# Attention and SwiGLU block on one core: the reciprocal of the softmax sums, on VectorE or on GpSimd by place in the program

## The chip, the cores and the metric

One core of a Trainium2 chip runs the whole program. The metric is the device time of one execution in microseconds, as a median over runs; lower is better. Engines are named as the profile names them: PE is TensorE, DVE is VectorE, ACT is ScalarE, POOL is GpSimd, SP is SyncE, which here only issues DMAs.

## The reference

A block with adaptive layer norm: 32-head softmax attention over 2048 tokens of width 512 (16 columns a head), then a SwiGLU feed-forward of width 1792.

```python
q, k, v = qkv[0], qkv[1], qkv[2]
scores = jnp.einsum("bhqd,bhkd->bhqk", q, k) * scale
p = _softmax(scores, axis=-1)
o = jnp.einsum("bhqk,bhkd->bhqd", p, v)
x = x + ga * (o.reshape(B, S, D) @ wo)
h = _layernorm(x, axis=-1) * (1 + cb) + sb
x = x + gb * ((_silu(h @ w_gate) * (h @ w_up)) @ w_down)
```

The change concerns one division: the row sum of the softmax, by which each row of `o` is divided.

## The kernel before

**Units and steps.** Attention is cut into 32 units (`NU`): unit `u` is one group of four heads against one chunk of 512 queries, eight units a chunk, four chunks. A unit has 16 steps, one per tile of 128 keys. In a step PE makes four score matmuls (`score`, L571), ACT turns each into exponentials (L573), and two steps later PE multiplies them with the values (`pv_step`, L586). The values carry a column of ones, so the sums of the softmax come out as a 17th row of each head's product. Ahead of the scores by 20 steps (`LEAD` is 21), PE makes four more score matmuls per step in the other orientation (`max_one`, L523), and DVE reduces each from PSUM to its row maximum (L525). They go over four banks in turn, so that PE can be some banks ahead of DVE and no more. After 64 of them `max_rows` (steps without filler) or `max_turned` (steps with filler) turns a unit's maxima into rows that are written into the unit's query operand by small DMAs from SP (`qop<-mr`, L541, or `qop<-turned`, L562); the first score of that unit reads them.

**Plain steps and steps with filler.** The program's order is written out by hand. `plain` emits steps that hold attention alone and sets `beside = False`; `filled` emits steps with matmuls of the previous chunk's output projection and feed-forward between those of attention (L789) and sets `beside = True`. Plain steps run from the beginning of attention to step 147, then around the chunk ends up to steps 275 and 403, in a stretch of 36 after the third chunk's output projection, and three at a time ahead of a chunk's last down projection.

**The end of a unit.** `close_unit` (L929) queues the division of a finished unit, one part per step:

- `out_a`, L597: SP sends the four rows of sums from `o` to `dn`, spread over 128 partitions by 16 columns.
- `out_b`, L601 and L602: DVE takes the reciprocal of `dn` in place; SP writes it to `d_dr` in DRAM.
- `out_r`, L607: SP reads `d_dr` back as `rb`, each row broadcast over 32 partitions. This DMA waits for the landing of the one before it.
- `out_c`, L613 and L614: POOL multiplies `o` by `rb` to `on` and sends it to `o_dr`.

All engines execute their own list in order, and so does SP: a DMA that waits for a semaphore holds back the DMAs behind it, `qop<-mr` of a later unit among them.

**POOL's other work.** In the first eight units POOL also splits the feed-forward's weights in two parts (`split_weights`, three pieces a unit, L644 to L686) and issues half of the loads of the key operand (`kop<-kd`) and of the query operand (`qop<-qd`) for the unit three ahead. In later units it makes the second parts of the hidden activations (L870, L871).

The steps of the end of a unit, as `close_unit` sets them:

```python
i0 = i if u % NG == NG - 1 else i + 3
at(i0 + 3, lambda: res.__setitem__(u, out_b(u, nc.sync, *res[u])))
at(i0 + 4, lambda: res.__setitem__(u, out_r(u, nc.sync, *res[u])))
at(i0 + 5, lambda: out_c(u, nc.gpsimd, nc.gpsimd, *res.pop(u)))
```

Of the kernel before, what the change touches and what calls it, by code (L numbers as in the profile page):

```python
# [11 lines left out]
F32 = mybir.dt.float32  # L12
# [4 lines left out]
ALU = mybir.AluOpType  # L17
# [4 lines left out]
P = 128  # L22
# [10 lines left out]
NU = NG * NC  # L33
# [70 lines left out]
def block_kernel(ctx, tc, x, wqkv, wo, w_gate, w_up, w_down, c, w_mod, out):  # L104
    nc = tc.nc
# [386 lines left out]
    pb = ctx.enter_context(tc.tile_pool(name="pb", bufs=2, reuse_waits="tile"))  # L492
# [100 lines left out]
    def out_a(u, eng):  # L593
# [3 lines left out]
        eng.dma_start(dn, o[16:P:32, :].rearrange("h (b e) -> h b e", e=16))  # L597
        return o, dn

    def out_b(u, eng, o, dn):  # L600
        nc.vector.reciprocal(dn, dn)  # L601
        eng.dma_start(d_dr[u].rearrange("h (b e) -> (h b) e", e=16), dn)  # L602
        return o,

# [324 lines left out]
    def close_unit(u, i):  # L929

        if u == NU - 1:
            res[u] = out_a(u, nc.scalar)
            return
        res[u] = out_a(u, nc.sync)
        if u + 3 < NU:
            load_k(u + 3)
            load_q(u + 3)
# [4 lines that stand above are left out]
        if u % NG == NG - 1:  # L942
            if u // NG:
                at(i + 4, lambda: begin(u // NG))
                at(i + 5, lambda: chunks[u // NG].load_wo())
            at(i + 7, lambda: chunks[u // NG].load_o(nc.gpsimd))
            at(i + 9, lambda: chunks[u // NG].split_o())
# [5 lines left out]
    beside = True  # L953
# [184 lines left out]
    for t in range(4):  # L1138
        out_terms(ch, t, banks[t], range(NK - 1))
    on = out_b(NU - 1, nc.scalar, *res[NU - 1])  # L1140
    on = out_r(NU - 1, nc.scalar, *on)
    out_c(NU - 1, nc.scalar, nc.vector, *on)
# [47 lines left out]
```

## Time and profile before

| What | Value |
|---|---|
| Median of 3 runs | 1826.32 us (1826.1 to 1827.04) |
| The profiled execution | 1826.86 us, its span 1825.0 us |
| PE busy | 1816.3 us (100%) |
| DVE busy | 1521.2 us (83%) |
| ACT busy | 1248.0 us (68%) |
| POOL busy | 459.9 us (25%) |
| Chain that ended last | PE 83%, DVE 14%, ACT 1% |
| Granted PE clock | 1.000 over the span |

Busy time of PE is modelled from pipelined matmuls and is an average over stages with different limits; the stage is read with the timeline, the waits and the busy time by window. A line such as L525 is a line of the kernel before.

### The profile page before, as it was taken

The page shows a single profiled execution, that of the slowest core. Times are in us where ns is not written, and L with a number is a line of the kernel's source. Part 1 is how long each engine was busy: PE and PEld are TensorE (multiplying, and loading weights), DVE is VectorE, ACT ScalarE, POOL GpSimd, SP SyncE. Part 2 cuts the span into 40 slices and gives each one's busy share as a digit, 9 for nine tenths or more (in the row PEclk, how much of TensorE's full clock was granted, in tenths as well). Part 3 has the DMA queues.
Part 4 walks back from the last instruction along what each step waited for, and adds up shares of the span by engine and source line. Part 5 has one row for each costly group of instructions (what it writes and reads, how often), then busy time and mean ns, then how long its engine had stood idle before and what let it go on. Part 6 is the DMA issues. An engine that isn't in the chain of part 4 may idle for free.

```text
span 1825.0 us, 40961 instructions
## 1 busy us (share of the span) xinstructions
PE 1816.3 (100%) x16904; PEld 1202.5 (66%) x16904; DVE 1521.2 (83%) x2554; ACT 1248.0 (68%) x2358; POOL 459.9 (25%) x538
## 2 busy tenths in 40 slices
PE   9999999999999999999999999999999999999999
PEld 7876444444465777776565777776564577777887
DVE  5578999999999888888999888889999988832544
ACT  4223888888888766777888767767888876673211
POOL 3612544556223111111123111111113011131200
PEclk9999999999999999999999999999999999999999
DMA  9883876667845444453544554444643536333742
GB/s 307 288 232 138 203 199 172 179 167 199 207 81 125 103 122 143 115 149 70 145 110 105 141 125 118 122 118 91 161 80 57 116 90 157 134 123 120 279 167 108
DMA packets 80486, 267.62 MB, mean 147 GB/s; under 512 B 19604, under 2 KB 24212, under 8 KB 59620
## 3 DMA queue, kind: packets, MB, share of 16 engines
q1 hardware_dynamic: 61324, 179.71, 34.0%
q0 software_dynamic: 18288, 84.49, 19.5%
q8 instruction: 133, 2.18, 0.5%
q10 hardware_dynamic: 688, 0.80, 0.1%
q14 instruction: 53, 0.43, 0.1%
HBM read 201.85 MB, written 62.13 MB: 145 GB/s over the span
## 4 chain that ended last, share of the span: by engine, by line
PE 83%; DVE 14%; ACT 1%; DMA 0%; issue 0%; SPq 0%; DVEq 0%
PE bank L586 21%; PE bank L789 20%; PE bank L571 14%; DVE mx L525 14%; PE bank L523 11%; PE bank L808 8%; PE bank L213 7%; PE bank L851 1%; PE bank L772 0%; DMA wm_ab<-in_w_mod 0%; PE bank L165 0%; ACT sq L832 0%; DVE v_flat L882 0%; PE bank L537 0%; SPq L261 0%
## 5 line engine op out<-in xcount | busy, mean ns | idle before, releaser
L525 DVE TENSOR_REDUCE mx<-bank 128x1 f32<-128x512 f32 x2048 | 1273.3, 681 | 111.0 <-PE bank L523 63.7
L571 PE MATMUL bank<-qop,kop 50*128 50x512 f32 x2048 | 729.7, 426 | 0.4 <-ACT pt__16494 L573 0.2
L523 PE MATMUL bank<-kop,qop 48*128 48x512 f32 x2048 | 724.6, 425 | 0.3
L571 PEld LDWEIGHTS bank<-qop,kop 50*128 50x128 f32 x2048 | 343.1, 184 | 168.9 <-issue 49.8
L523 PEld LDWEIGHTS bank<-kop,qop 48*128 48x128 f32 x2048 | 342.8, 184 | 106.2 <-DVE mx L525 62.1
L789 PE MATMUL bank<-act,wgu 64*128 64x512 f32 x1872 | 303.5, 392 | 0.0
L789 PEld LDWEIGHTS bank<-act,wgu 64*128 64x128 f32 x1872 | 199.4, 187 | 22.5
L613 POOL TENSOR_TENSOR on<-o,rb 128x512 f32<-128x512 f32 x31 | 39.9, 1286 | 507.8 <-DMA rb<-d_dr 359.0
L789 PE MATMUL bank<-wd,mid 64*128 64x512 f32 x912 | 131.6, 391 | 0.0
L870 POOL CAST mid<-m 128x512 fp32r<-128x512 f32 x40 | 24.4, 609 | 380.5 <-DVE m L868 273.7
L789 PEld LDWEIGHTS bank<-wd,mid 64*128 64x128 f32 x912 | 92.2, 186 | 11.2
L213 PE MATMUL bank<-hT,wqs 128*128 128x512 f32 x384 | 94.4, 397 | 0.4 <-DVE wqs L353 0.4
L866 DVE SCALAR_TENSOR_TENSOR q<-th,bank 128x512 f32<-128x512 f32 x56 | 38.3, 683 | 54.2 <-ACT th L862 54.2
L213 PEld LDWEIGHTS bank<-hT,wqs 128*128 128x128 f32 x384 | 70.6, 188 | 19.1 <-issue 3.2
L862 ACT ACTIVATE th<-bank 128x512 f32<-128x512 f32 x56 | 33.2, 594 | 57.9 <-PE bank L808 57.9
L882 DVE TENSOR_TENSOR x<-bank,x 128x512 f32<-128x512 f32 x84 | 53.9, 685 | 16.1 <-PE bank L789 16.1
L868 DVE TENSOR_TENSOR m<-bank,q 128x512 f32<-128x512 f32 x56 | 38.7, 692 | 21.7 <-PE bank L808 19.7
L871 POOL TENSOR_TENSOR mid<-m,mid 128x512 fp32r<-128x512 f32 x40 | 51.7, 1292 | 3.3
L808 PE MATMUL bank<-wd,mid 128*128 128x512 f32 x216 | 51.3, 393 | 0.0
L213 PE MATMUL bank<-wqs,hT 128*128 128x512 f32 x192 | 48.0, 398 | 0.0
L789 PE MATMUL bank<-wgu,act 64*128 64x512 f32 x288 | 47.6, 392 | 0.0
L808 PEld LDWEIGHTS bank<-wd,mid 128*128 128x128 f32 x216 | 40.4, 188 | 8.9
(6300 smaller groups left out, 5137.3 us busy)
## 6 DMA issues: line engine op xcount, KB each, us to landing
wgu<-gu_dr SPq DMA_DIRECT2D x48, 1024.0 KB
wd<-wd_dr SPq DMA_DIRECT2D x28, 1024.0 KB
kop<-kd SPq DMA_DIRECT2D x33, 768.0 KB
kop<-kd POOLq DMA_DIRECT2D x29, 768.0 KB, 8.8
gu_dr<-wgu POOLq DMA_DIRECT2D x14, 1024.0 KB, 13.6
kd<-prt SPq DMA_DIRECT2D x16, 512.0 KB
qd<-prt SPq DMA_DIRECT2D x16, 512.0 KB
kop<-gu_dr SPq DMA_DIRECT2D x8, 1024.0 KB
```

Source lines behind the costliest of these rows:

```text
L213: nc.tensor.matmul(pt, lhs(a, k), rhs(b, k), start=(n == 0), stop=(n == 3 * nk - 1))
L523: nc.tensor.matmul(pm, qop[u][rows, s, qt * P:(qt + 1) * P], kop[u % 3][rows, s, kc * CW:(kc + 1) * CW], start=True, stop=True)
L525: nc.vector.tensor_reduce(mx[u][:, b, s, qt, kc:kc + 1], pm, op=ALU.max, axis=AX.X)
L571: nc.tensor.matmul(sp, kop[u % 3][rows, h // 2, kt * P:(kt + 1) * P], qop[u][rows, h // 2, :], start=True, stop=True)
L586: nc.tensor.matmul(pv[u][32 * h:32 * h + 32, cols], v_flat[:, e0:e0 + 32], p_[h][:, cols], start=(kt == 0 and half == 0), stop=(kt == 15), ...
L613: mul.tensor_mul(on, o, rb)
L789: mm = nc.tensor.matmul(outs[e], lhs(e, a, k)[rows], rhs(b, k)[rows], start=(ph == 0 and j == 0), stop=(j == z and (ph == 1 or trade)), sk ...
L808: nc.tensor.matmul(outs[e], lhs(e, a, k), rhs(b, k), start=(j == 0), stop=(j == z))
L866: nc.vector.scalar_tensor_tensor(q, th, 1.0, outs[0], op0=ALU.add, op1=ALU.mult)
L868: nc.vector.tensor_mul(m32, outs[1], q)
L871: (nc.gpsimd if slow else nc.vector).tensor_sub(mid[:, 1, :], m32, mid[:, 0, :].bitcast(F32))
L882: nc.vector.tensor_add(ch.x2[:, t, :], outs[e], ch.x2[:, t, :])
```

## The change

In the changed program `out_b` has two branches. Where the unit's reciprocal falls in a step with filler, and for the last unit, DVE takes it as before. Where it falls in a plain step, POOL makes it in four instructions: a power of -1, and one Newton step (a product, `2 - product`, a product). A tile of exponents is filled once.

```diff
+    power = pb.tile([P, 16], F32, name="power", bufs=1)
+    nc.gpsimd.memset(power, -1.0)
+
     def out_b(u, eng, o, dn):
-        nc.vector.reciprocal(dn, dn)
+        if beside or u == NU - 1:
+            nc.vector.reciprocal(dn, dn)
+        else:
+            near, off = [pb.tile([P, 16], F32, name=f"near{k}", tag=f"near{k}", bufs=1) for k in range(2)]
+            nc.gpsimd.tensor_tensor(near, dn, power, op=ALU.pow)
+            nc.gpsimd.tensor_mul(off, dn, near)
+            nc.gpsimd.tensor_scalar(off, off, -1.0, 2.0, op0=ALU.mult, op1=ALU.add)
+            nc.gpsimd.tensor_mul(dn, near, off)
         eng.dma_start(d_dr[u].rearrange("h (b e) -> (h b) e", e=16), dn)
         return o,
```

Fourteen of the 32 reciprocals go to POOL: units 0 to 7, 14, 15, 22, 23, 25 and 26. From L602 on, lines carry numbers 10 higher in the changed program (L613 is L623). Three places show what moves.

DVE's list at the end of unit 0, as a piece of the difference (`bank_63` to `bank_66` are the banks of the maxima):

```order
 L525 TENSOR_REDUCE mx<-bank_64 128x1
 L525 TENSOR_REDUCE mx<-bank_65 128x1
-L601 RECIPROCAL dn<-dn 128x16
 L525 TENSOR_REDUCE mx<-bank_63 128x1
 L525 TENSOR_REDUCE mx<-bank_66 128x1
```

The reciprocal goes; the reductions around it keep their order.

POOL's list at the same place, before (the last store of a split weight, the division of unit 0, the next piece of weights):

```order
L652 DMA gu_dr<-wgu 128x2048
L613 TENSOR_TENSOR on<-o,rb 128x512
L614 DMA o_dr<-on 128x512
L644 DMA mid<-in_B_w_up 128x4x256
L686 TENSOR_TENSOR mid<-mid,gb_bc 128x1024
```

and in the changed program:

```order
L662 DMA gu_dr<-wgu 128x2048
L608 TENSOR_TENSOR near_2180<-dn,power 128x16
L609 TENSOR_TENSOR near_2181<-dn,near_2180 128x16
L610 TENSOR_SCALAR near_2181<-near_2181 128x16
L611 TENSOR_TENSOR dn<-near_2180,near_2181 128x16
L623 TENSOR_TENSOR on<-o,rb 128x512
L624 DMA o_dr<-on 128x512
L654 DMA mid<-in_B_w_up 128x4x256
L696 TENSOR_TENSOR mid<-mid,gb_bc 128x1024
```

The four instructions stand behind the weights of the unit and ahead of its division; nothing else on POOL moves.

SP's list at the end of unit 6, with the semaphores that each DMA waits for, before:

```order
L602 DMA d_dr<-dn 128x16 [waits DMAHW2_49,DVE_49]
L607 DMA rb<-d_dr 128x1x512 [waits DMAHW4_49,DMAHW2_49,Pool_49]
L541 DMA qop<-mr 2x8x128 [waits Activation_49]
L541 DMA qop<-mr 2x8x128 [waits DMAHW5_49]
```

and in the changed program:

```order
L612 DMA d_dr<-dn 128x16 [waits DMAHW2_49,Pool_49]
L617 DMA rb<-d_dr 128x1x512 [waits DMAHW4_49,DMAHW2_49]
L541 DMA qop<-mr 2x8x128 [waits Activation_49]
L541 DMA qop<-mr 2x8x128 [waits DMAHW5_49]
```

No DMA moves; the write of the reciprocals now waits for POOL where it waited for DVE, and the rows of maxima of unit 8 stand two DMAs behind it.

## Rows read from the trace of the kernel before

**Rows 1.** Busy time by window: us, PE, PEld, DVE, ACT, POOL busy (instructions), PEclk, DMA share, GB/s.

```profile
225.00:433.00 208.00, 207.94 (x2106) 100.86 (x2104) 207.81 (x357) 181.92 (x360) 102.19 (x105) 1.00 0.71 188
433.00:520.00 87.00, 86.95 (x884) 42.13 (x880) 86.80 (x150) 75.95 (x153) 37.61 (x39) 1.00 0.63 165
...
878.00:931.00 53.00, 52.80 (x543) 25.34 (x543) 52.83 (x90) 45.52 (x90) 15.09 (x20) 1.00 0.63 149
...
1283.00:1337.00 54.00, 53.80 (x536) 27.50 (x537) 53.27 (x91) 46.83 (x92) 14.00 (x18) 1.00 0.66 152
1394.00:1458.00 64.00, 63.90 (x641) 32.90 (x645) 63.22 (x109) 55.38 (x109) 6.04 (x8) 1.00 0.38 87
```

**Rows 2.** Waits in the plain stretch 225 to 520: us in total, times, longest.

```profile
PEld bank L523 <- DVE mx L525: 30.8, 89, 0.4
```

**Rows 3.** Timeline of DVE around unit 0's reciprocal: start us, us, engine, instruction.

```profile
231.01 0.24 DVE L601 RECIPROCAL dn<-dn 128x16 f32<-128x16 f32 x1
231.17 10.78 DVE L525 TENSOR_REDUCE mx<-bank 128x1 f32<-128x512 f32 x18
...
242.00 28.78 DVE L525 TENSOR_REDUCE mx<-bank 128x1 f32<-128x512 f32 x48
```

**Rows 4.** Chain of work through 225 to 350: start us, us, what.

```profile
231.09 0.16 DVE dn L601
```

**Rows 5.** Timeline of DVE around unit 14's reciprocal, in three plain steps between filled ones.

```profile
862.62 0.24 DVE L601 RECIPROCAL dn<-dn 128x16 f32<-128x16 f32 x1
862.78 5.68 DVE L525 TENSOR_REDUCE mx<-bank 128x1 f32<-128x512 f32 x9
868.70 2.06 DVE L525 TENSOR_REDUCE mx<-bank 128x1 f32<-128x512 f32 x3 [0.24 <-PE bank L523]
```

**Rows 6.** Timeline of POOL at the ends of units 0, 5 and 6.

```profile
223.35 0.59 POOL L652 DMA_DIRECT2D gu_dr<-wgu  x1 [0.30 <-POOL wgu L649]
240.90 1.27 POOL L613 TENSOR_TENSOR on<-o,rb 128x512 f32<-128x512 f32 x1 [16.96 <-DMA rb<-d_dr]
...
422.00 0.59 POOL L652 DMA_DIRECT2D gu_dr<-wgu  x1 [0.30 <-POOL wgu L649]
...
465.88 2.37 POOL L686 TENSOR_TENSOR mid<-mid,gb_bc 128x1024 f32<-128x1024 f32 x1 [6.42 <-DMA mid<-in_B_w_down]
...
472.12 0.60 POOL L652 DMA_DIRECT2D wd_dr<-wd  x1 [0.30 <-POOL wd L649]
476.40 1.28 POOL L613 TENSOR_TENSOR on<-o,rb 128x512 f32<-128x512 f32 x1 [3.69 <-DMA rb<-d_dr]
```

**Rows 7.** Timeline of POOL in a chain of small instructions (a layer norm's scale).

```profile
1370.14 0.20 POOL L755 TENSOR_TENSOR rs<-rs,mv 128x4 f32<-128x4 f32 x1
1370.44 0.20 POOL L756 TENSOR_SCALAR rs<-rs 128x4 f32<-128x4 f32 x1
```

**Rows 8.** Timeline of SP's DMAs at the ends of units 0, 5 and 6.

```profile
214.89 0.61 SPq L597 DMA_DIRECT2D dn<-o  x1
...
424.80 0.34 SPq L602 DMA_DIRECT2D d_dr<-dn  x1
432.82 0.56 SPq L607 DMA_DIRECT2D rb<-d_dr  x1
437.50 1.12 SPq L541 DMA_DIRECT2D qop<-mr  x2
...
463.17 0.34 SPq L602 DMA_DIRECT2D d_dr<-dn  x1
470.65 0.56 SPq L607 DMA_DIRECT2D rb<-d_dr  x1
477.12 1.40 SPq L541 DMA_DIRECT2D qop<-mr  x2
```

**Rows 9.** Score matmuls up to 481.2: count, ns min/median/max, first and last start.

```profile
L571 PE MATMUL bank<-qop,kop x513: 383/398/503, 167.5 to 480.9; 50*128 50x512 f32 x171
```

**Rows 10.** The dn tile, whole span: what its engine idled for, us, times.

```profile
  DMA dn<-o: 7.0, 1
```

## Prediction

> **What bounds the kernel now.** I read the page first, then the busy time by window, then DVE's timeline at each reciprocal. The page says PE 100% and DVE 83%, and its chain is mostly PE; that is an average over two kinds of stages. The windows tell them apart: from 225 to 433 us DVE is busy 207.81 of 208.00 us, and it is nearly as full in the other four windows of plain steps, 86.80 of 87, 52.83 of 53, 53.27 of 54 and 63.22 of 64 [rows 1]. PE reads as full in the same windows, but its ends are modelled; that it waits for DVE shows in the waits, where the weight load ahead of the matmul for the maxima stood 89 times behind a reduction between 225 and 520 us, 30.8 us in all [rows 2]. In plain steps, then, DVE sets the pace, at one reduction per 0.60 us (48 in 28.78 us) [rows 3]. In steps with filler PE sets it.
>
> What to see around unit 0's reciprocal: it starts at 231.01 us, and the next reduction at 231.17 us [rows 3]. Its 0.24 us of busy time overlap its neighbours, and it takes 0.16 us of DVE's time; the chain through this stretch also gives it 0.16 us [rows 4].
>
> **What the change removes.** Fourteen reciprocals leave DVE. Each is worth 0.16 us where DVE is the bound. By DVE's timeline that holds for twelve: units 0 to 7 lie in the first two windows, 15 and 23 in the next two, 25 and 26 in the last [rows 1]. Units 14 and 22 end in three plain steps between filled ones; there DVE runs out of work and waits 0.24 us for PE soon after unit 14's reciprocal [rows 5], and unit 22 repeats it. I count these two at nothing: PE hides them. So 12 x 0.16 = 1.92 us. PE is next in line in plain steps, and 0.16 us in a unit of some 38.5 us (64 reductions and two small instructions) is far less than what it waits for DVE per unit (30.8 us over 295 us, some 4 us a unit, of which a part overlaps matmuls in flight), so it does not take the gain back.
>
> **What it adds on POOL.** Four instructions on 128x16. For three of them the nearest rows are POOL's chain on 128x4: 0.20 us each, 0.30 us from start to start [rows 7]; the 128x512 product took 1.27 us [rows 6], so twelve more columns add 12 x (1.27 - 0.20) / 508 = 0.03 us. That makes 1.0 us for three. No row shows a power. Its lower bound is a product's 0.3 us; for the upper I take the 1.27 us of the product over 32 times the columns, though no row excludes more (a rival below). I take 0.5 us, nearer the 128x4 row because the tile is nearer to it: 1.5 us in all, between 1.3 and 2.3.
>
> This lies beside other work. After unit 0's last store, issued by 223.94 us, POOL did nothing until 240.90 us: it waited 16.96 us for `rb` [rows 6]. DVE came to the reciprocal at 231.01 us; POOL can begin it when the sums have landed, which is after their issue at 214.89 [rows 8] and, as DVE never waited for them but once at the very end of the program [rows 10], before 231.01. So the write of the reciprocals can leave up to 5.5 us sooner than before. At unit 5 POOL is free at 422.59 us, and done at 424.1 us, where SP issued at 424.80 [rows 6, 8]: no earlier, no later. The sooner division lets POOL begin the next unit's weights sooner, until the key loads wait for PE to let go of a buffer. It ends nothing that PE or DVE waits for, so I count it at nothing.
>
> The Trainium skill, GPSIMD Engine Reference, section 4.1, speaks against the move: elementwise work belongs on VectorE, since GpSimd is about twice as slow on two inputs. By that as a price for the path, four instructions at twice 0.24 us, fourteen times, would cost an estimated 27 us less the 2 saved; by the idle time in the rows it costs nothing.
>
> **The tight place is unit 6.** There POOL first waited 6.42 us for the last piece of weights, and was done with it only at 472.72 us, while DVE had let the reciprocals go at 463.17 us [rows 6, 8]. POOL's four instructions would end near 474.2 us, and the write would leave 11.3 us later than before. SP waits for its landing, which took 7.5 us from issue (463.17 to 470.65), then issues the read and only then the rows of maxima for unit 8. With the same landing time these leave at 474.5 + 7.5 + 0.6 = 482.6 us instead of 477.12 [rows 8]. The 513th score matmul, the first of unit 8, started at 480.9 us [rows 9], 2.4 us after the second of those DMAs was issued, and the landing takes part of that. So PE could stall by up to 5.5 us. Two things stand against it. If POOL enters unit 6 sooner by some 3 us (each earlier end sends its division 0 to 5.5 us sooner), 2.5 us are left; and DVE has filled banks to go on with, three at 0.6 us. I take 0 and keep 5.5 us for the range.
>
> **The sum.** 1826.86 us for the profiled execution less 1.92 is 1824.94. The median of the runs lies 0.54 us under that execution, so I forecast **1824.4 us**. That is 0.1%, and less than the 0.2% (3.65 us) that a measurement of this kernel can about tell from no change.
>
> **Rivals.**
>
> *Unit 6 is late.* For it: the 11.3 us above. Against it: POOL's head start. Price 1 to 5.5 us off the gain: 1825.4 to 1829.9, with 1827 as its middle.
>
> *Another bound takes over.* PE or ACT needs the 0.16 us itself, and DVE idles instead. For it: PE 207.94 of 208.00 us and the chain's share of PE. Against it: the waits for DVE. Time: 1826.3.
>
> *The power is slow, and the kernel slower than before.* The mechanism is one queue: a long power holds POOL, SP stands at the write of the reciprocals, and the rows of maxima behind it leave late, so that PE waits for the first score of a unit. At unit 5 the write could leave at 437.50 - 0.56 - 8.02 = 428.9 us without harm, 6.0 us after POOL is free (the 8.02 us are 424.80 to 432.82) [rows 6, 8]; unit 6 has nothing to spare. From about 6 us for the four instructions, unit 6 alone costs more than the change brings by over 3.65 us (10 us late, less 2 to 3 us that banks and head start absorb). At 10 us, unit 6 costs some 12 us, unit 5 some 3 and units 2 to 4 about 1 each: 18 - 1.9 gives 1842. Against it: the tile has only 16 columns. For it: no row shows a power on POOL, and one computed element by element could take this long. The Trainium skill, GPSIMD Engine Reference, section 2.1, adds that the first call of freshly loaded code pays about 6 us; no run here shows that for a power, paid once at unit 0 it would hide in the 17 us of idle time, and paid at every call it would make this rival true.
>
> *More than the sum.* Units 14 and 22 count too and each is worth its whole 0.24 us: 14 x 0.24 = 3.4 us, 1822.9; or the earlier divisions help somewhere I don't see.
>
> **How the numbers follow.** The forecast has a chance of 0.60, a late unit 6 of 0.17, another bound 0.10, the slow power 0.10, more than the sum 0.03. The range leaves out the slow power and a little of the others: from 1822.6 (the 3.4 us, and 0.3 us for the spread of runs) to 1829.4 (nearly all of unit 6's 5.5 us). Faster by over 0.2% needs a gain above 3.65 us, which only the last rival could give, with the edge of a noisy result: 0.04. Slower by over 0.2% is the slow power and a sliver of a late unit 6 with a cost that I undersized: 0.11. Within 0.2%: 0.85.
>
> **What would show it.** Right: in the changed profile 18 reciprocals of this tile remain on DVE, the reductions next to the removed ones follow at 0.6 us, DVE stays full in the plain windows, and the span from unit 0's end to unit 8's first score is shorter by 8 x 0.16 = 1.3 us, the rest being saved later. The four POOL instructions take 1.3 to 2.3 us. Wrong in the way of unit 6: the first score of unit 8 waits for `qop<-mr`, and DVE shows a gap of more than 1 us near 482 us. Wrong in the way of the power: one row on POOL of several us in each of the fourteen units, and waits for `qop<-mr` ahead of scores. If DVE shows new idle times after each removed reciprocal, another bound took over. If the time moves by more than 5.5 us with none of this, the prediction is wrong in a way that I have not seen.

## The result, and the profile after

The changed kernel takes 1834.38 us (median of six runs, 1832.39 to 1835.35) against 1826.99 us for the kernel before (six runs, 1826.1 to 1828.79): a ratio of 1.0038, 95% interval 1.0025 to 1.005. The change makes it slower by some 7 us. I had forecast 1824.4 us in a range up to 1829.4, so the time lies outside, on the side that I held unlikely. The profiled execution took 1832.39 us with a span of 1830.3 us; it is the fastest of the six.

On the page of the changed kernel (columns as described with its parts 1 and 5: busy us, share, instructions; then busy us, mean ns, idle before and its releaser):

```profile
PE 1817.3 (99%) x16904; PEld 1194.8 (65%) x16904; DVE 1521.1 (83%) x2540; ACT 1247.9 (68%) x2358; POOL 509.9 (28%) x595
...
L571 PE MATMUL bank<-qop,kop 50*128 50x512 f32 x2048 | 729.1, 425 | 3.6 <-DMA qop<-mr 3.1
...
L608 POOL TENSOR_TENSOR near<-dn,power 128x16 f32<-128x16 f32 x14 | 41.1, 2938 | 39.7 <-DMA dn<-o 39.6
```

PE fell from 100% of its span to 99%. Fourteen powers cost POOL 41.1 us, 2.94 us each. And the scores, L571, have an idle time that ended with `qop<-mr`: one wait of 3.1 us, the one that I had named as the sign of a late unit 6.

**Where the time went.** I subtracted the start of each instruction in the trace before from that of the same instruction in the trace after. This offset says in which stretch time was lost or won:

| Stretch of the changed kernel | Offset at its start | At its end |
|---|---|---|
| start to 20 us | 0 | +1.78 us |
| 20 to 464 us, units 0 to 5 | +1.78 | +0.92 |
| 464 to 494 us, end of unit 6, first scores of unit 8 | +0.92 | +5.55 |
| 494 to 1652 us | +5.55 | +4.52 |
| 1652 us to the end | +4.52 | +5.3 |

So the gain is there: 0.86 us over six units and 1.03 us in the rest, 1.9 us in all. Two places lose far more: the end of unit 6, 4.6 us, and the first 20 us of the program, 1.8 us. A further 0.8 us goes at the very end. DVE shows the gain as it was meant; in a plain stretch of the changed kernel (start us, us, instruction) its reductions run on where a reciprocal stood between them [rows 3]:

```profile
281.31 37.75 DVE L525 TENSOR_REDUCE mx<-bank 128x1 f32<-128x512 f32 x63
```

63 reductions in 37.75 us are 0.60 us each, with no gap.

**Unit 6.** POOL's timeline of the changed kernel at the ends of units 0 and 6 (last column: idle before, and its releaser) answers to [rows 6]:

```profile
225.54 2.96 POOL L608 TENSOR_TENSOR near<-dn,power 128x16 f32<-128x16 f32 x1
228.58 0.22 POOL L609 TENSOR_TENSOR near<-dn,near 128x16 f32<-128x16 f32 x1
228.90 0.20 POOL L610 TENSOR_SCALAR near<-near 128x16 f32<-128x16 f32 x1
229.19 0.22 POOL L611 TENSOR_TENSOR dn<-near,near 128x16 f32<-128x16 f32 x1
241.18 1.28 POOL L623 TENSOR_TENSOR on<-o,rb 128x512 f32<-128x512 f32 x1 [11.76 <-DMA rb<-d_dr]
...
466.19 2.37 POOL L696 TENSOR_TENSOR mid<-mid,gb_bc 128x1024 f32<-128x1024 f32 x1 [5.56 <-DMA mid<-in_B_w_down]
...
473.04 2.95 POOL L608 TENSOR_TENSOR near<-dn,power 128x16 f32<-128x16 f32 x1
...
476.67 0.22 POOL L611 TENSOR_TENSOR dn<-near,near 128x16 f32<-128x16 f32 x1
```

At unit 0 the four instructions take 3.9 us (225.54 to 229.41) and lie in idle time. At unit 6 POOL is held up by a load of weights, comes to the power at 473.04 us, and ends at 476.89. SP's timeline there, to be read beside [rows 8]:

```profile
476.92 0.34 SPq L612 DMA_DIRECT2D d_dr<-dn  x1
478.41 0.56 SPq L617 DMA_DIRECT2D rb<-d_dr  x1
479.03 1.13 SPq L541 DMA_DIRECT2D qop<-mr  x2
```

The write leaves 13.75 us later than before (463.17), its landing is waited for only 1.5 us instead of 7.5, and the rows of maxima leave 1.9 us later than before (477.12). Now they stand right behind the read `rb`, and the chain through this stretch shows what that does to them (start us, us, what):

```profile
479.63 5.28 DMA qop<-mr
484.92 0.14 issue
485.05 0.46 PE bank L571
```

They need 5.28 us from the issue of the second of them, and the first score of unit 8 starts at 485.05 us, where it started at 480.9 before [rows 9]. What follows stands in the windows (PE, PEld, DVE, ACT, POOL busy, then the granted clock, DMA share, GB/s). The kernel before:

```profile
10.00:20.00 10.00, 8.49 (x55) 5.26 (x54) 6.12 (x16) 6.20 (x11) 1.28 (x1) 1.00 0.94 302
...
484.00:488.00 4.00, 4.00 (x42) 2.11 (x40) 4.00 (x8) 3.80 (x9) 0.00 (x0) 1.00 1.10 331
```

and the changed one:

```profile
10.00:20.00 10.00, 8.70 (x48) 5.27 (x49) 3.90 (x12) 4.47 (x8) 1.27 (x1) 0.83 0.75 231
...
480.00:484.00 4.00, 1.98 (x22) 0.71 (x20) 3.27 (x6) 2.39 (x5) 0.00 (x0) 1.00 0.64 190
484.00:488.00 4.00, 2.95 (x22) 1.50 (x24) 0.69 (x1) 0.60 (x1) 1.54 (x2) 0.71 0.96 389
488.00:492.00 4.00, 4.00 (x32) 1.54 (x30) 3.85 (x7) 3.57 (x8) 1.55 (x3) 0.86 0.81 182
```

PE stands for 3.1 us, and behind the wait its granted clock is 0.71 and 0.86 over two windows, where it was 1.00; windows of 1 us add up to 3.4 us at 0.50, that is at 1.2 instead of 2.4 GHz. Of the 4.63 us lost here, 3.2 are lost when the first score starts (485.05 - 480.9 - 0.92), the other 1.4 after it.

**The start.** The first row of both fences is the other place: clock 1.00 before, 0.83 after. PE's timeline before,

```profile
1.19 9.05 PE L275 MATMUL bank<-busy 128*128 128x256 f32 x28 [1.19 <-DVE nil L278]
10.87 1.06 PE L286 MATMUL bank<-wm_ab,sc 128*32 128x512 f32 x8 [0.63 <-DMA wm_ab<-in_w_mod]
```

and after:

```profile
1.18 7.88 PE L275 MATMUL bank<-busy 128*128 128x256 f32 x28 [1.18 <-DVE nil L278]
11.12 1.89 PE L286 MATMUL bank<-wm_ab,sc 128*32 128x512 f32 x8 [2.06 <-DMA wm_ab<-in_w_mod]
```

L275 are matmuls that only keep PE busy until the first weights arrive (14 in the source, 28 in the trace). They ended 1.2 us sooner, PE then stood for 2.06 us, and the next eight matmuls took 1.89 us instead of 1.06.

### The profile page after: what moved, and what is told of

Same layout as the page of the kernel before. It is cut to its first block, busy times and chain, and to the rows that moved or that the text cites. A ratio compares the mean times of both kernels' runs of the same rounds, so it can differ in the third digit from the quotient of the medians.

```text
span 1830.3 us, 41008 instructions
## 1 busy us (share of the span) xinstructions
PE 1817.3 (99%) x16904; PEld 1194.8 (65%) x16904; DVE 1521.1 (83%) x2540; ACT 1247.9 (68%) x2358; POOL 509.9 (28%) x595
## 4 chain that ended last, share of the span: by engine, by line
PE 88%; DVE 8%; ACT 2%; DMA 2%; issue 0%; SPq 0%; DVEq 0%; ACTq 0%
PE bank L586 24%; PE bank L799 20%; PE bank L571 16%; PE bank L523 13%; DVE mx L525 8%; PE bank L213 7%; PE bank L818 7%; PE bank L782 0%; DMA wm_ab<-in_w_mod 0%; PE bank L165 0%; DMA qop<-mr 0%; DMA kop<-o_dr 0%; DMA rb<-d_dr 0%; ACT sq L842 0%; PE bank L861 0%
## 5 line engine op out<-in xcount | busy, mean ns | idle before, releaser
L571 PE MATMUL bank<-qop,kop 50*128 50x512 f32 x2048 | 729.1, 425 | 3.6 <-DMA qop<-mr 3.1
L571 PEld LDWEIGHTS bank<-qop,kop 50*128 50x128 f32 x2048 | 343.5, 184 | 175.5 <-issue 54.1
L623 POOL TENSOR_TENSOR on<-o,rb 128x512 f32<-128x512 f32 x31 | 39.9, 1288 | 413.2 <-DMA rb<-d_dr 316.4
L608 POOL TENSOR_TENSOR near<-dn,power 128x16 f32<-128x16 f32 x14 | 41.1, 2938 | 39.7 <-DMA dn<-o 39.6
```

Source lines behind the costliest of these rows:

```text
L571: nc.tensor.matmul(sp, kop[u % 3][rows, h // 2, kt * P:(kt + 1) * P], qop[u][rows, h // 2, :], start=True, stop=True)
L608: nc.gpsimd.tensor_tensor(near, dn, power, op=ALU.pow)
L623: mul.tensor_mul(on, o, rb)
```

## The experiments

Each ratio is to the kernel before, timed beside it, with its 95% interval. Edits are against the changed kernel unless the text says otherwise.

**The kernel before, again** (no edit to it).

> The kernel before, unchanged, to see what a measurement of no change looks like and how far the start of the program moves from one execution to the next. Theory Q (the loss is one queue at unit 6): ratio 1.000, its interval within 0.999 to 1.001; the first score matmul starts anywhere between 167 and 170 us, since the 1.7 us by which the changed program was late there are spread. Rival S (the changed program itself starts later, by 1.7 us in every execution): the first score of the copy starts at 167.5 us within 0.3 us.

Measured: 1826.65 against 1826.74 us, 0.9998 [0.999 to 1.0007]; clock 1.00 throughout, first score of the program at 166.9 us (169.2 in the changed kernel). A ratio can be told from 1 to about 0.1%. Between 20 and 1652 us this copy's offset moves by 0.4 us with no edit at all, so a gain of 1.9 us read from offsets is good to about half a microsecond. The first score lies outside what either theory had named.

**Unit 6 back on DVE.**

```diff
-        if beside or u == NU - 1:
+        if beside or u in (6, NU - 1):
```

> The change with unit 6 put back on DVE; thirteen reciprocals stay on POOL. Theory Q: no score waits for qop<-mr, PE's clock stays at 1.00 around 485 us, and eleven reciprocals of 0.16 us are saved: 1.8 us less than before, ratio 0.999. Rival S: about 1 us more than before, ratio 1.0005. Rival P (reciprocals on POOL cost time wherever they are made): still 4 us or more slower, ratio above 1.002.

Measured: 1825.48 against 1826.74 us, 0.9993 [0.9984 to 1.0002]. No score waits for `qop<-mr`, the write leaves at 462.27 us, the first score of unit 8 starts at 480.0. With one of the fourteen back on DVE the whole loss is gone; the other thirteen leave about 1 us of gain, not clear of no change. The start is not late here either, which the edit does not explain.

**Only unit 6 on POOL.**

```diff
-        if beside or u == NU - 1:
+        if u != 6:
```

> Unit 6 alone on POOL; the other 31 reciprocals stay on DVE. Theory Q: the whole loss is here, 4 to 6 us slower than before, ratio 1.0022 to 1.0033, with a wait of PE for qop<-mr of 3 us or more at the first score of unit 8 and a lower granted clock behind it. Rival P: a fourteenth of the loss, ratio within 1.000 to 1.001. Rival S: 2 us slower at most.

Measured: 1831.67 against 1826.74 us, 1.0026 [1.0013 to 1.0039]; the seven runs go from 1826.64, no loss at all, to 1836.87, which is the profiled one. Its chain:

```profile
474.23 2.97 POOL near L608
...
478.12 1.44 DMA d_dr<-dn
...
479.58 0.56 SPq L617
...
480.19 0.56 SPq L541
...
480.80 4.98 DMA qop<-mr
...
485.92 0.76 PE bank L571
```

This is the whole path in one piece: power, write, read, rows of maxima, score. And its windows:

```profile
484.00:488.00 4.00, 2.08 (x18) 0.91 (x18) 0.69 (x1) 0.60 (x1) 1.26 (x1) 0.65 0.98 373
488.00:492.00 4.00, 4.00 (x26) 1.83 (x20) 1.92 (x4) 1.65 (x4) 1.82 (x3) 0.50 0.73 213
492.00:496.00 4.00, 4.00 (x26) 1.44 (x28) 3.33 (x6) 3.54 (x7) 0.00 (x0) 0.50 1.02 156
496.00:500.00 4.00, 4.00 (x36) 1.72 (x30) 2.29 (x4) 1.70 (x4) 0.00 (x0) 0.64 1.07 154
```

The wait is 5.3 us; behind it PE runs at 0.50 of its clock for two whole windows and parts of two more, 13.7 us in all. The offset jumps by 10.7 us, twice the wait.

**Unit 6's write and read issued from POOL's queue.**

```diff
+        queue = nc.gpsimd if u == 6 else nc.sync
-        at(i0 + 3, lambda: res.__setitem__(u, out_b(u, nc.sync, *res[u])))
-        at(i0 + 4, lambda: res.__setitem__(u, out_r(u, nc.sync, *res[u])))
+        at(i0 + 3, lambda: res.__setitem__(u, out_b(u, queue, *res[u])))
+        at(i0 + 4, lambda: res.__setitem__(u, out_r(u, queue, *res[u])))
```

> The change, with the write d_dr<-dn and the read rb<-d_dr of unit 6 issued from POOL's queue instead of SP's; the four instructions on POOL stay where they are, as late as in the change. Theory Q: SP no longer stands at the write, the rows of maxima leave at about 478 us, no score waits, and 1.9 us are saved: ratio 0.999. Rival L (POOL's lateness itself is the loss, through the key loads and the division behind it, not SP's queue): a loss of 4 us or more stays, ratio above 1.002.

Measured: 1826.81 against 1826.74 us, 1.0 [0.9991 to 1.0009]. SP's timeline:

```profile
477.13 1.09 SPq L541 DMA_DIRECT2D qop<-mr  x2
```

The division of unit 6 itself is even later than in the change (its product at 489.15 us against 484.61), but the rows of maxima leave as in the kernel before, at 477.13, and no score waits. So nobody needs the quotient soon; what hurts is what stands behind it on SP. The 1.9 us that were to be saved besides do not show in the ratio.

**Only the read moved to POOL's queue.** In the last line of the program above, `nc.gpsimd if u == 6 else nc.sync` for `out_r` alone.

> The change, with the read rb<-d_dr of unit 6 alone issued from POOL's queue; the write stays on SP, behind POOL's four instructions, so SP stands there as long as in the change. Theory R (the rows of maxima are late because the read stands ahead of them on SP's queue and its transfer has to end first): they leave at about 479 us as before, land within 2.5 us, PE waits less than 1 us, ratio 0.999 to 1.000. Theory Q' (SP's wait for POOL at the write is what makes them late): PE waits over 2 us, ratio 1.002 or more.

Measured: 1827.25 against 1826.62 us, 0.9999 [0.9991 to 1.0008]. SP's timeline:

```profile
475.00 0.34 SPq L612 DMA_DIRECT2D d_dr<-dn  x1
475.79 1.10 SPq L541 DMA_DIRECT2D qop<-mr  x2
```

No score waits and the clock stays at 1.00. This run changes two things, however. The rows were to leave at about 479 us, as late as in the change, and left at 475.79, sooner than in the kernel before (477.12): POOL was done 1.9 us sooner here, and SP no longer waits for the landing of the write. So the run alone does not say whether the rows suffer from leaving late or from the read ahead of them.

The DMA packets in the traces do. The rows are 32 packets of 512 B. Here they moved at 476.96 to 477.77 us, and in the kernel before, whose read was through at 475.92, at 478.31 to 479.40: within 2.3 us of the first issue. In the changed kernel, issued at 479.03, they moved at 482.69 to 483.97, when most of the read's 128 packets of 2 KB (479.76 to 483.44) were through. So of the 4.6 us by which the rows come later than before, 1.9 are a later issue and 2.7 are spent behind the read, which broadcasts each row of reciprocals to 32 partitions and stands ahead of them on the same queue. In all five profiles in which a score waits, the chain shows 5.0 to 5.3 us for the rows.

**A short instruction in place of the power.** This kernel leaves out the power, so its quotients are wrong.

```diff
-            nc.gpsimd.tensor_tensor(near, dn, power, op=ALU.pow)
+            nc.gpsimd.tensor_tensor(near, dn, power, op=ALU.mult)
```

> The change with the power replaced by a product of the same shape, so that the reciprocals are wrong and the four instructions take 1.2 us instead of 3.9. Theory Q1 (the 2.9 us of the power are what makes unit 6 too late): the write leaves near 474 us, the rows of maxima of unit 8 leave no later than before, PE waits less than 1.5 us for them, and the time is 0 to 2 us under the kernel before: ratio 0.999 to 1.000. Theory Q2 (POOL's lateness at unit 6, done with the weights at 473 us, is enough by itself): PE still waits over 1.5 us at the first score of unit 8, ratio 1.001 or more.

Measured: 1831.45 against 1827.32 us, 1.0018 [1.0008 to 1.0028]. The four instructions now end at 473.73 us, 3.2 us sooner. SP:

```profile
473.75 0.34 SPq L612 DMA_DIRECT2D d_dr<-dn  x1
478.14 0.56 SPq L617 DMA_DIRECT2D rb<-d_dr  x1
478.76 1.13 SPq L541 DMA_DIRECT2D qop<-mr  x2
```

The write's landing is waited for 4.4 us instead of 1.5, so the rows of maxima leave only 0.27 us sooner, take 5.00 us, and the score waits 2.4 us:

```profile
PE bank L571 <- DMA qop<-mr: 2.4, 1, 2.4
```

By the packets, the write now meets POOL's store of the last piece of weights: the store's move until 477.46 us and the write's until 477.51; in the change the store was through at 477.81, 0.9 us behind the issue of the write. The length of the power is not the cause; a POOL that is free, and a store that leaves, only at some 472 us are.

**The last piece of weights behind the division.** Of the last three pieces of weights that POOL splits, the third starts four steps later (against the kernel with the change).

```diff
-(1, 3, 5)):
+(1, 3, 9)):
```

> The change with the last piece of the split weights moved behind the end of unit 6 (steps 1, 3 and 9 instead of 1, 3 and 5), so that POOL comes to unit 6's reciprocal near 461 us instead of 473. All fourteen reciprocals stay on POOL, at their full 3.9 us. Theory Q: the write leaves near 465 us, no score waits, 1.9 us are saved: ratio 0.999. Rival (the power costs time at the other units too): ratio 1.000 or more.

Measured: 1826.33 against 1827.32 us, 0.9994 [0.9986 to 1.0003]; all fourteen on POOL, no wait, the write at 463.03 us.

> The kernel with all fourteen reciprocals on POOL and the last piece of the split weights behind the end of unit 6, timed a second time, since 0.1% is near what the first timing could tell. Theory Q: 1.0 to 1.9 us less than the kernel before, ratio 0.999 to 0.9995. Rival: no difference, ratio 0.9998 to 1.0005.

Measured, the same kernel again: 1825.47 us (eleven runs, 1824.92 to 1826.68) against 1827.62 us (1826.05 to 1831.01), 0.9988 [0.998 to 0.9997]. SP's timeline has the spacing of the kernel before again:

```profile
463.35 0.34 SPq L612 DMA_DIRECT2D d_dr<-dn  x1
470.84 0.56 SPq L617 DMA_DIRECT2D rb<-d_dr  x1
476.35 1.13 SPq L541 DMA_DIRECT2D qop<-mr  x2
```

This version beats the changed kernel clearly, and its medians lie under the kernel before by 1.0 and 2.2 us, about the forecast gain of 1.9 us and below the 0.2% that I had set as a bound; only the second of the two intervals excludes no change.

**The power twice, unit 6 on DVE.** This asks whether a long power alone makes the kernel slow.

```diff
+            nc.gpsimd.tensor_tensor(near, dn, power, op=ALU.pow)
             nc.gpsimd.tensor_tensor(near, dn, power, op=ALU.pow)
```

> The change with unit 6 on DVE and the power made twice at the thirteen others, 6.8 us for the five instructions. The prediction on record put the point from which unit 5 delays SP at 6.0 us. Theory Q: SP's rows of maxima at units 0 to 5 have 4 us or more in hand after the single power (at unit 5 the read leaves at 434.0 and the rows at 438.5), so 2.9 us more delay no score: ratio 0.999, as with the power made once. The prediction's rival: a wait for qop<-mr appears at unit 7's first score, ratio 1.001 or more.

Measured: 1826.02 against 1827.32 us, 0.9993 [0.9984 to 1.0001]. At unit 5, POOL:

```profile
420.20 2.95 POOL L608 TENSOR_TENSOR near<-dn,power 128x16 f32<-128x16 f32 x1
423.22 2.90 POOL L609 TENSOR_TENSOR near<-dn,power 128x16 f32<-128x16 f32 x1
...
426.81 0.23 POOL L612 TENSOR_TENSOR dn<-near,near 128x16 f32<-128x16 f32 x1
```

and SP:

```profile
427.06 0.34 SPq L613 DMA_DIRECT2D d_dr<-dn  x1
433.96 0.56 SPq L618 DMA_DIRECT2D rb<-d_dr  x1
436.91 1.13 SPq L541 DMA_DIRECT2D qop<-mr  x2
```

6.8 us of division cost nothing: the write left 2.3 us later than before [rows 8], the rows of maxima 0.6 us sooner. But POOL began here at 420.20 us, before the 422.59 us at which it was free in the kernel before, so the write left ahead of the 428.9 us from which the prediction expected harm at unit 5. That limit was not reached, and so not tested.

**No reciprocal in the fourteen units** (the others keep theirs; the edit is against the kernel before).

```diff
-        nc.vector.reciprocal(dn, dn)
+        if beside or u == NU - 1:
+            nc.vector.reciprocal(dn, dn)
```

> The kernel before with the fourteen reciprocals left out altogether, so that these units are multiplied by their sums instead of divided: the most that taking them off DVE can give. Theory Q: twelve times 0.16 us, 1.9 us, ratio 0.999, and nothing behind the sums waits. Rival (another bound takes over part of it): 1 us or less, ratio 0.9995 or more.

Measured: 1826.04 against 1827.32 us, 0.9992 [0.9983 to 1.0001]. The most that the idea can give measures 1.3 us, with an interval that holds both no change and the forecast 1.9 us; it is of the size of the gain in the versions without the stall.

**The changed kernel again.**

> The change, unchanged, timed again. Theory Q: the loss is the stall at unit 6 and the clock behind it, 4 to 9 us, less 1.9: ratio 1.002 to 1.004; the 1.7 us at the start of the program and the 0.8 us near its end that the first profile showed are spread and need not be there. Rival S (the changed program starts late in every execution): first score after 169 us again, granted clock below 1.00 between 10 and 20 us.

Measured: 1835.95 against 1826.62 us (five runs, 1833.39 to 1838.36), 1.0045 [1.0031 to 1.0058]. The same two places again: 10 to 20 us at a clock of 0.83, and a wait of 4.8 us at unit 8's first score, with

```profile
484.00:488.00 4.00, 0.47 (x2) 0.32 (x2) 0.00 (x0) 0.00 (x0) 0.95 (x1) 0.76 0.96 315
488.00:492.00 4.00, 4.00 (x28) 1.62 (x30) 1.72 (x3) 1.66 (x4) 2.12 (x4) 0.50 0.76 308
492.00:496.00 4.00, 4.00 (x26) 1.65 (x20) 2.75 (x5) 2.62 (x6) 0.00 (x0) 0.50 1.02 185
```

behind it. Here the offset jumps by 10.0 us, where the first profile showed 4.63. The first score of the program starts at 169.9 us: the late start, which I had expected not to return, did. The stall is in both profiles, its price varies, and that first profile was a cheap case; that its time, 5.5 us over before's profile, lies under the medians' 7.4 fits this. All eleven times of the changed kernel (1832.39 to 1838.36 us) lie above every time of the kernel before (at most 1831.04).

**More matmuls ahead of the first weights.**

```diff
-    for i in range(14):
+    for i in range(18):
```

> The change with 18 instead of 14 of the matmuls on constants that keep PE busy until its first weights land (L275; nothing reads their result). In both profiles of the change PE idled 2.1 and 2.8 us there, its clock fell for 3.4 us, and the first score started at 169.2 and 169.9 us instead of 167.5. Theory C (that start is one more idle gap of PE with a fall of its clock behind it): the gap closes, the clock stays up between 10 and 20 us, the first score starts at 167 to 168 us and the ratio falls by about 0.001, to 1.003; the stall at unit 6 stays. Rival D (the data lands later, and the clock has nothing to do with it): the first score stays after 169 us.

Measured: 1832.37 against 1827.62 us, 1.0027 [1.0014 to 1.0039]. At the start, PE:

```profile
1.17 9.55 PE L275 MATMUL bank<-busy 128*128 128x256 f32 x36 [1.17 <-DVE nil L278]
10.99 1.06 PE L286 MATMUL bank<-wm_ab,sc 128*32 128x512 f32 x8 [0.27 <-DMA wm_ab<-in_w_mod]
```

The gap falls to 0.27 us, the eight matmuls are back at 1.06 us, and the program's first score starts at 167.4 us, 1.8 us sooner than in the changed kernel. Unit 6 still waits, 4.0 us. So the two losses are separate. The ratio is lower than the change's 1.0038 and 1.0045, but the intervals overlap; the 1.8 us are read from the trace.

## Why the prediction was wrong

**The step that failed** stands in "The tight place is unit 6": "I take 0 and keep 5.5 us for the range." The first half of that paragraph was right: POOL late with the weights, the write late behind it, SP held, the first score of unit 8 waiting for `qop<-mr`. The two things that I set against it do not hold.

- *POOL's head start of some 3 us.* It was to come from divisions that end sooner, and little came of them. At unit 0 the write left at 229.44 us instead of 231.28, but the landing behind it took 6.9 us instead of 4.6, and the read left at 236.36 instead of 235.93: about 1 us sooner, if the 1.5 us are taken off by which the whole program was late there. At unit 5 nothing was left: the product began at 439.32 us instead of 438.19, with the program 1.0 us late. In unit 6 POOL came to its last piece of weights at 460.63 us (466.19 less its wait of 5.56) instead of 459.46, with 0.9 us to take off: no sooner. And that piece waits for a load, so that POOL would only have waited longer.
- *Filled banks.* They feed DVE. The engine that stands is PE, whose list is in order and which had no spare time there: 4.00 of 4.00 us busy in the window before.

**The size of the stall** came from three sizes, all off, and not to the same side. The write was to leave at 474.5 us and left at 476.92; its landing was to take 7.5 us and took 1.5; the score was to follow 2.4 us after the second of the rows of maxima was issued, and followed 4.9 us after (485.05 against 480.16), since the rows' packets came last behind the read's. The errors nearly cancel, and the upper bound of 5.5 us holds for the waits, 2.4 to 5.3 us.

**The price of the stall** was the term that I had not seen: behind a wait PE's clock is at 0.50 for a while, and that can cost as much as the wait or more. The five profiles with a wait at unit 8's first score:

| Profile | PE waits | Clock at 0.50 | Offset jumps by |
|---|---|---|---|
| short instruction | 2.4 us | 10.2 us | 6.6 us |
| the change | 3.1 us | 3.4 us | 4.6 us |
| more matmuls at the start | 4.0 us | 6.8 us | 6.0 us |
| the change again | 4.8 us | 13.7 us | 10.0 us |
| only unit 6 on POOL | 5.3 us | 13.7 us | 10.7 us |

What is lost beyond the wait follows the time at half clock, not the length of the wait: some 0.4 us for each microsecond that PE worked at 0.50. With this, the rival "unit 6 is late" (1825.4 to 1829.9) was the right case with too small a price. The same effect at the start was not in my list at all.

**The power** was mis-sized: 2.93 us (median of the fourteen) where I took 0.5 between 0.3 and 1.27, and 3.9 us for the four instructions against 1.3 to 2.3. The other three, at 0.20 to 0.22 us, were right. But a power of 0.23 us leaves the kernel at 1.0018, and one of twice the length, kept away from unit 6, at 0.9993. So the rival of the slow power had the right path, one queue and late rows, but not the right cause: at unit 6 the four instructions did harm at 3.9 us and even at 1.1, under the 6 us that I had set, and at unit 5 none at 6.8 us, where POOL began sooner. The Trainium skill, GPSIMD Engine Reference, section 2.1, tells of some 6 us for the first call of freshly loaded code; the first power here began 0.02 us behind the store before it and took 2.96 us, against a median of 2.93, so no such payment shows. The price estimated by the Trainium skill, the same page, section 4.1 (27 us for fourteen), shows in no time either: POOL's busy time rose by 50 us, but in thirteen of the units that work is hidden.

**What held.** Twelve times 0.16 us: 1.9 us won by the offsets. By the medians it is less sure: the versions with all moves that wait for nothing lie between 0.6 us above the kernel before (only the read moved) and 2.2 us under it (weights behind, again), and of their intervals only the last excludes no change. DVE as the bound of plain steps: no new idle time beside its reductions in the stretch shown, so nothing speaks for "another bound takes over". Nor does anything for "more than the sum": without any reciprocal in these units the gain is 1.3 us.

**What stays open.** Why the start is late: it was so in three profiles (the change, its repeat, the short instruction) and in none of the other ten with the same 14 matmuls in L275. What goes with it is the moment at which these matmuls speed up from one per 0.43 us to one per 0.22: at 4.4 to 4.8 us in the three late profiles, at 5.0 to 7.3 us in the ten others. The sooner they speed up, the sooner the block ends (it takes 7.88 to 9.33 us) and the longer PE stands before the first weights. Why that moment differs is not shown, and as PE's list is the same up to there, chance is not excluded. The other open point is the 0.8 us at the very end, in the DMAs of the last unit's division, which four profiles have (the change, its repeat, unit 6 on DVE, the power twice); the others lose at most 0.4 us there. No run was made for it.

## What to carry to other kernels

Before moving work to an idle engine, find the busiest place at which it lands, and read there which DMA waits for it and what stands behind that DMA on its queue: thirteen of fourteen moves were free, and one cost more than all could bring. Do not count on a head start of an engine that a load releases, nor on an earlier issue landing earlier. A stall of TensorE in a full stretch cost one and a half to nearly three times its length here. Moving one piece of other work by four steps turned a loss of 0.4% into a gain of about 0.1%, which one of its two timings tells from no change.

## What the runs showed of the hardware

- A wait of PE of 2.4 to 5.3 us in a stretch where it had been full came with a granted clock of 0.50 (1.2 of 2.4 GHz) for 3.4 us (the changed kernel's first profile) to 13.7 us (its repeat, and only unit 6 moved); the shortest wait had 10.2 us of it. At the start, gaps of 2.06 to 2.75 us (the change, the short instruction, the repeat) were followed by eight matmuls in 1.75 to 1.93 us; a gap of 1.72 us (write and read on POOL's queue) by the same eight in 1.07 us.
- The first matmuls of the program run at two rates, one per 0.43 us and then one per 0.22, as at 1.2 and 2.4 GHz. The trace holds no clock record until the rate changes (4.39 us in the changed kernel, 6.77 in the kernel before), so the 1.00 that a window prints there is no reading. In the kernel before, the 28 took 9.05 us, in the changed one 7.88, and 36 took 9.55. Their end, not the weights' arrival (10.87 and 11.12 us), makes most of the difference between the gaps.
- A DMA of a few KB can take as long as what stands ahead of it on its queue: the rows of maxima landed in 5.0 to 5.3 us behind the broadcast read, and moved within 2.3 us of their issue where none stood just ahead.
- A small write's landing belongs to the moment: that of unit 6's reciprocals was waited for 7.5 us at 463.17 us, with a store from POOL in flight (its packets move from 464.28 to 471.04), 4.4 us at 473.75 (store to 477.46), and 1.5 us at 476.92, 478.12 and 479.66, where the store was through or all but. A later issue need not be a later arrival. No run moved that store alone.
- A power on POOL takes 2.93 us for 128x16, a product of the same size 0.22.
